# Local attention's later units computed in pairs that share PSUM banks

## The chip, the cores and the metric

The kernel runs on one NeuronCore of a Trainium2 chip, as one program. TensorE (PE) multiplies matrices into PSUM, VectorE (DVE) and ScalarE (ACT) work on PSUM and SBUF, and SyncE (SP) issues nearly all DMA transfers from one queue. The metric is the device time of one execution in microseconds (us); lower is better.

## The reference

Three parts follow each other. The first is attention of 4 batches with 8 heads of width 64, over 512 local positions and 32 global ones:

```python
    s_ll = scale * np.matmul(q_l, k_l.transpose(0, 1, 3, 2))
    mask = np.abs(pos[:, None] - pos[None, :]) <= window      # window = 32
    s_ll = np.where(mask, s_ll, -1000000000.0)
    s_lg = scale * np.matmul(q_l, k_g.transpose(0, 1, 3, 2))
    a_l = sm(np.concatenate([s_lg, s_ll], axis=-1))
    out_l = np.matmul(a_l, np.concatenate([v_g, v_l], axis=2))
```

Beside it 32 global queries see all 544 keys. Its output, 2176 rows of 512, goes through two layers of the same form, `g(x @ w_in) @ w_out` with an inner width of 2048: the first with a leaky activation, the second with `h * relu6(h + 3) / 6`. Everything is in float32.

## The kernel before

**Local units.** A unit is a batch, half of the positions and a pair of heads: 32 units, in the order batch, half, pair of heads. `scores(u)` (L192) multiplies 32 queries at a time by a window of 128 keys, for two heads; heads lie on partitions 0 to 63 and 64 to 127, so these matmuls use 64 rows and 32 columns of the array. The scores of one head go to one PSUM bank (`s0_ps`, `s1_ps`), half of whose 512 columns a unit fills. DVE reads them with the mask and the minimum (L200, four reads a unit), ACT takes the exponential (L204, four a unit), DVE makes the reciprocal of the sums (L206, L208). `transposes(u)` (L215) turns the four 128x128 tiles on PE into one bank, and ACT copies it to `pt` (L217). `values(u)` (L227) multiplies by the values with 128 rows and 32 columns of the array into half of a bank `o_ps`, and DVE scales the result into `xo` (L231). A program's matmul in float32 shows in the trace as two: 16 in the order are 32 in the profile.

**The loop.** `local_units` is a generator. Up to unit 3, and from unit 4 to the last, step k does the transposes of unit k-1 and gives control back; then the scores of unit k, the values of unit k-2, the loads of q and k (L172, L174) for unit k+2 and of v (L179) for unit k+1, and gives control back again. `v_t` has 3 buffers, `q_t` and `k_t` have 4, `p` 2, `xo` 8.

**What runs beside it.** The main program goes through five blocks of rows of the first layer (512, 512, 512, 256 and 384 rows). A block's step s multiplies for `h` (L373), then takes one or two steps of the generator, then multiplies for `y` (L404) with the `g` of two steps earlier; `act` makes `t` and `g` on ACT and DVE (L383, L385, L391, L392). At the end of a block the outputs `xo` of the next block's units are transposed into `xt` (L358, L344, L345), and `y` goes to DRAM (L946, L947, L949). In the first block, which runs in two lanes of 256 columns, the first layer's weights are converted from raw 64-bit words as they come in (L97, L112, L116, L120, L122, L128, L129, mostly DVE); in the blocks after it those of the second layer (`second_weights`, L469 to L501, loads at L97, stores at L478). After the local units the global ones (`global_units`) use the same memory: their loads (`gq`, `gk`, `gv`, L274 to L282) wait until the local units have let go of it.

**Order.** The code is written in that order, and a scheduler with a timeline model places the instructions on each engine; every engine then takes its instructions in that fixed order. PSUM has two pools of four banks; from the first block on, `y_ps` has one pool, and `h_ps`, `s_ps`, `pt_ps`, `o_ps` and `xt_ps` take turns in the other.

## Time and profile before

| | us |
|---|---|
| median of 3 runs (861.42 to 865.12) | 864.32 |
| the profiled execution | 862.99 |
| its span, from the first instruction to the last | 861.2 |
| PE busy in the span | 836.2 |
| DVE busy | 592.5 |
| ACT busy | 418.6 |
| granted TensorE clock, mean share of full speed | 0.986 |

The span lies 1.8 us under the time of the same execution. Busy time of PE counts a matmul from its start to its modelled end, and matmuls overlap; the distance between the starts of two groups tells what a group costs. In the chain of work that ended last each piece is the time that it adds.

### The profile page before, as it was taken

The numbers are of one execution on the slowest core, as the hardware profiler recorded it, in microseconds if no ns is written. First come the engines' busy times: TensorE is split into PE (matmuls) and PEld (weight loads), VectorE is DVE, ScalarE is ACT, GpSimd is POOL, SyncE is SP. The second block draws the span as 40 slices with busy tenths as digits, with TensorE's granted clock in tenths as the row PEclk, the third lists the DMA queues.
The fourth block names the chain that finished last, engine by engine and source line by source line (L and its number), as shares of the span: only waits on it lengthen the run. The fifth ranks groups of instructions, "written<-read, shape, count | busy, mean of one in ns | idle before, by whom it ended". The sixth has DMA issues, their size and how long they took to land.

```text
span 861.2 us, 18367 instructions
## 1 busy us (share of the span) xinstructions
PE 836.2 (97%) x7232; PEld 746.6 (87%) x7232; DVE 592.5 (69%) x1321; ACT 418.6 (49%) x905; POOL 0.2 (0%) x4
## 2 busy tenths in 40 slices
PE   8899999999999999989999999999999999999997
PEld 5678989878778788878999998879999998999996
DVE  4889987566767776677779837779854786854221
ACT  5777665555555555455546523335532343442222
POOL 0000000000000000000000000000000000000000
PEclk7899999999999999999999999999999999999999
DMA  8885664357667656599678626768666887888872
GB/s 309 305 283 181 232 206 139 114 171 249 215 231 246 253 191 210 204 339 327 221 275 286 232 93 220 227 206 275 186 207 217 288 298 222 283 258 262 296 250 77
DMA packets 75204, 199.90 MB, mean 232 GB/s; under 512 B 7792, under 2 KB 23920, under 8 KB 74096
## 3 DMA queue, kind: packets, MB, share of 16 engines
q1 hardware_dynamic: 75024, 198.61, 69.5%
q8 instruction: 57, 0.93, 0.5%
q14 instruction: 27, 0.22, 0.1%
q10 hardware_dynamic: 96, 0.13, 0.1%
HBM read 156.25 MB, written 42.47 MB: 231 GB/s over the span
## 4 chain that ended last, share of the span: by engine, by line
PE 82%; DVE 7%; DMA 6%; ACT 3%; issue 1%; SPq 1%; ACTq 0%
PE h_ps L373 18%; PE y_ps L404 17%; PE o_ps L802 16%; PE k_ps L722 15%; DMA raw<-in_w 4%; PE h_ps L869 4%; PE o_ps L660 4%; PE s_ps L192 2%; PE pt_ps L215 2%; DVE z L120 1%; PE o_ps L227 1%; DMA ws<-wo 1%; DVE z L122 1%; DVE t L385 1%; ACT raw L112 1%
## 5 line engine op out<-in xcount | busy, mean ns | idle before, releaser
L404 PE MATMUL y_ps<-g,wt 128*128 128x256 f32 (+2 forms) x1152 | 212.3, 334 | 5.7 <-ACT g L391 4.0
L373 PE MATMUL h_ps<-xt,wt 128*128 128x256 f32 (+2 forms) x1152 | 209.9, 332 | 3.3 <-ACT wt L128 1.9
L404 PEld LDWEIGHTS y_ps<-g,wt 128*128 128x128 f32 x1152 | 175.3, 189 | 26.5 <-ACT g L391 4.6
L373 PEld LDWEIGHTS h_ps<-xt,wt 128*128 128x128 f32 x1152 | 179.3, 192 | 21.3 <-ACT wt L128 2.1
L802 PE MATMUL o_ps<-ws,gh 128*128 128x256 f32 x784 | 141.5, 284 | 3.3 <-DMA ws<-wo 3.0
L722 PE MATMUL k_ps<-bt,ws 128*128 128x512 f32 (+1 forms) x672 | 137.8, 364 | 0.0
L722 PEld LDWEIGHTS k_ps<-bt,ws 128*128 128x128 f32 x672 | 121.9, 190 | 12.7
L802 PEld LDWEIGHTS o_ps<-ws,gh 128*128 128x128 f32 x784 | 121.9, 192 | 4.8 <-DMA ws<-wo 3.7
L802 PE MATMUL o_ps<-ws,gl 128*128 128x256 f32 x392 | 108.6, 284 | 0.0
L772 DVE TENSOR_TENSOR gl<-far,gh 128x1024 fp32r<-128x1024 f32 (+1 forms) x56 | 60.7, 1088 | 38.5 <-ACT gh L771 38.1
L771 ACT CAST gh<-far 128x1024 fp32r<-128x1024 f32 (+1 forms) x56 | 52.4, 941 | 63.7 <-PE o_ps L802 53.3
L385 DVE SCALAR_TENSOR_TENSOR t<-t,c_sb,h_ps 128x256 f32<-128x256 f32 (+2 forms) x96 | 55.2, 587 | 40.8 <-ACT t L383 40.7
L802 PEld LDWEIGHTS o_ps<-ws,gl 128*128 128x128 f32 x392 | 74.3, 192 | 0.2
L383 ACT ACTIVATE t<-h_ps 128x512 f32<-128x512 f32 (+2 forms) x84 | 42.9, 512 | 56.9 <-PE h_ps L373 55.3
L112 ACT ACTIVATE raw<-raw,quarter_sb 128x512 uint32<-128x512 uint32 x64 | 49.7, 778 | 25.9 <-DMA raw<-in_w 25.8
L391 ACT CAST g<-t 128x512 fp32r<-128x512 f32 (+2 forms) x84 | 44.9, 536 | 34.1 <-DVE t L385 32.1
L392 DVE TENSOR_TENSOR g<-t,g 128x512 fp32r<-128x512 f32 (+2 forms) x84 | 48.9, 584 | 18.2 <-ACT g L391 17.8
L707 ACT ACTIVATE t<-far,half_sb 128x512 f32<-128x512 f32 (+1 forms) x48 | 32.2, 670 | 49.2 <-DVE far L703 49.0
L204 ACT ACTIVATE p<-p,st 128x128 f32<-128x128 f32 x128 | 49.9, 391 | 11.3 <-DVE st L200 10.9
L120 DVE SCALAR_TENSOR_TENSOR z<-z,raw 128x512 uint32<-128x512 uint32 x64 | 43.8, 689 | 3.8 <-ACT raw L112 2.4
L122 DVE SCALAR_TENSOR_TENSOR z<-raw,z 128x512 uint32<-128x512 uint32 x64 | 43.5, 687 | 0.7
L869 PE MATMUL h_ps<-xt,ws 128*128 128x384 f32 x192 | 36.0, 336 | 0.0
(104 smaller groups left out, 880.9 us busy)
## 6 DMA issues: line engine op xcount, KB each, us to landing
ws<-wi SPq DMA_DIRECT2D x80, 512.0 KB, 4.7
ws<-wo SPq DMA_DIRECT2D x72, 512.0 KB, 4.3
raw<-in_w SPq DMA_DIRECT2D x64, 512.0 KB, 5.5
v_t<-in_vE SPq DMA_DIRECT2D x32, 512.0 KB, 5.5
wi<-raw SPq DMA_DIRECT2D x16, 512.0 KB, 3.2
wi<-parts SPq DMA_DIRECT2D x16, 512.0 KB, 5.2
wo<-raw SPq DMA_DIRECT2D x16, 512.0 KB, 3.9
wo<-parts SPq DMA_DIRECT2D x16, 512.0 KB, 4.8
```

The costliest lines, as they stand in the source:

```text
L112: here(nc.scalar.activation(low, low, AF.Relu, bias=quarter_sb, scale=0.9 * 2.0 ** -29))
L120: nc.vector.scalar_tensor_tensor(out=bits, in0=bits, scalar=3, in1=low, op0=ALU.logical_shift_left, op1=ALU.bitwise_or)
L122: nc.vector.scalar_tensor_tensor(out=bits, in0=high, scalar=0x80000000, in1=bits, op0=ALU.bitwise_and, op1=ALU.bitwise_or)
L204: nc.scalar.activation(p[:, n, :], p[:, n, :], AF.Exp, bias=st[:, 1, n:n + 1], scale=-1.0, accum_out=st[:, 2, n:n + 1])
L373: nc.tensor.matmul(ps[:, a:b], lhsT=wts[j][:, 0, wl, 128 * c:128 * c + 128], rhs=xt[c][:, xl, a:b], start=k == 0, stop=k == 3 * NC - 1)
L385: nc.vector.scalar_tensor_tensor(out=t[:, c:d], in0=t[:, c:d], scalar=c1_sb[:, j:j + 1], in1=ps[:, c:d], op0=ALU.mult, op1=ALU.add)
L404: nc.tensor.matmul(y[c][:, a:b], lhsT=wts[j][:, 1, wl, 128 * c:128 * c + 128], rhs=g[:, gl, a:b], start=first, stop=last)
L722: nc.tensor.matmul(bank, lhsT=wt[:, wl, at:at + 128], rhs=bt[x][:, c, xl, 0:w], start=first and k == 0, stop=k == 5, skip_group_check=True)
L771: nc.scalar.copy(hi, src)
L772: nc.vector.tensor_tensor(out=lo, in0=src, in1=hi.bitcast(F32), op=ALU.subtract)
L802: nc.tensor.matmul(bank, lhsT=part[:, jp, 128 * c:128 * c + 128], rhs=wo[:, jp, 256 * wl:256 * wl + 256], start=opens, stop=k == NP // 2 - ...
L869: nc.tensor.matmul(h, lhsT=wt[:, wl, 128 * c:128 * c + 128], rhs=xt[c][:, xl, 0:w], start=k == 0, stop=k == 3 * NC - 1)
```

## The change

The first eight units stay single: the second loop now ends at unit 8 (`SINGLE`), with its last units finished before the next begin. From unit 8 on the units go in twelve pairs. `scores` takes two units: the first unit's scores go to columns 0 to 255 of the two banks, the second's to columns 256 to 511, and all 32 matmuls of the program stand together; the two softmaxes follow. `values` takes two units in the same way, with both results in one bank. A pair takes four steps of the generator: the transposes of the pair before in the first, nothing in the second, the scores of this pair and the values of the one before in the third, the loads in the fourth (v of this pair, q and k of the next). Per engine the number of instructions stays the same, but for q and k of units 10 and 11, which the second loop loads and the first pair loads again. Two units use five banks where they used eight.

```diff
--- before.py
+++ after.py
@@ -33,6 +33,7 @@
 AHEAD = 2
 PRE = 3
 FIRST_UNITS = HP
+SINGLE = 2 * HP
 SKEW = 1
 ZB = 2
 WARM = 8
@@ -178,19 +179,25 @@
             v_t[u] = att.tile([128, 8, 2, D], F32, tag="vE", name="v_t", bufs=3)
             nc.sync.dma_start(out=v_t[u], in_=vE[b, hp, :, 8 * hf:8 * hf + 8])
 
-        def scores(u):
+        def scores(*us):
+            s = [bank("s0_ps"), bank("s1_ps")]
+            for e, u in enumerate(us):
+                b, hf, hp = units[u]
+                q, k = q_t.pop(u), k_t.pop(u)
+                for i in range(2):
+                    for g in range(4):
+                        at = 128 * i + W * g
+                        o = W * (start_of(8 * hf + 4 * i + g) - 12 * hf)
+                        to = 256 * e + 128 * i
+                        for h in range(2):
+                            rows = slice(64 * h, 64 * h + 64)
+                            nc.tensor.matmul(s[h][W * g:W * g + W, to:to + 128], lhsT=q[rows, at:at + W],
+                                             rhs=k[rows, o:o + 128], start=True, stop=True)
+            for e, u in enumerate(us):
+                softmax(u, [x[:, 256 * e:256 * e + 256] for x in s])
+
+        def softmax(u, s):
             b, hf, hp = units[u]
-            q, k = q_t.pop(u), k_t.pop(u)
-
-            s = [bank("s0_ps"), bank("s1_ps")]
-            for i in range(2):
-                for g in range(4):
-                    at = 128 * i + W * g
-                    o = W * (start_of(8 * hf + 4 * i + g) - 12 * hf)
-                    for h in range(2):
-                        rows = slice(64 * h, 64 * h + 64)
-                        nc.tensor.matmul(s[h][W * g:W * g + W, 128 * i:128 * i + 128], lhsT=q[rows, at:at + W],
-                                         rhs=k[rows, o:o + 128], start=True, stop=True)
             p = att.tile([128, 4, 128], F32, tag="p", name="p", bufs=SKEW + 1)
             st = att.tile([128, 4, 4], F32, tag="st", name="st", bufs=4)
             for i in range(2):
@@ -216,22 +223,25 @@
             pt_t[u] = att.tile([128, 4, 128], F32, tag="pt", name="pt", bufs=2)
             nc.scalar.copy(pt_t[u], t.rearrange("p (n q) -> p n q", n=4))
 
-        def values(u):
-            b, hf, hp = units[u]
-            pt, v, rs = pt_t.pop(u), v_t.pop(u), rs_t.pop(u)
+        def values(*us):
             o = bank("o_ps")
-            for i in range(2):
-                for h in range(2):
-                    n = 2 * i + h
-                    for g in range(4):
-                        nc.tensor.matmul(o[W * g:W * g + W, D * n:D * n + D],
-                                         lhsT=pt[:, n, W * g:W * g + W], rhs=v[:, 4 * i + g, h, :],
-                                         start=True, stop=True)
-            x = outs.tile([128, 2, 128], F32, tag="xo", name="xo", bufs=8)
-            nc.vector.tensor_tensor(out=x.rearrange("p i (h d) -> p (i h) d", h=2),
-                                    in0=o[:, 0:256].rearrange("p (n d) -> p n d", n=4),
-                                    in1=rs[:, :, None].to_broadcast([128, 4, D]), op=ALU.mult)
-            xo[b, hf, hp] = x
+            for e, u in enumerate(us):
+                pt, v = pt_t.pop(u), v_t.pop(u)
+                for i in range(2):
+                    for h in range(2):
+                        n = 2 * i + h
+                        to = 256 * e + D * n
+                        for g in range(4):
+                            nc.tensor.matmul(o[W * g:W * g + W, to:to + D],
+                                             lhsT=pt[:, n, W * g:W * g + W], rhs=v[:, 4 * i + g, h, :],
+                                             start=True, stop=True)
+            for e, u in enumerate(us):
+                b, hf, hp = units[u]
+                x = outs.tile([128, 2, 128], F32, tag="xo", name="xo", bufs=8)
+                nc.vector.tensor_tensor(out=x.rearrange("p i (h d) -> p (i h) d", h=2),
+                                        in0=o[:, 256 * e:256 * e + 256].rearrange("p (n d) -> p n d", n=4),
+                                        in1=rs_t.pop(u)[:, :, None].to_broadcast([128, 4, D]), op=ALU.mult)
+                xo[b, hf, hp] = x
 
 
 
@@ -246,7 +256,7 @@
         load_v(1)
         load_v(2)
         yield
-        for lo, hi in ((0, FIRST_UNITS), (FIRST_UNITS, n)):
+        for lo, hi in ((0, FIRST_UNITS), (FIRST_UNITS, SINGLE)):
             if lo:
                 load(lo)
                 load_v(lo)
@@ -264,6 +274,24 @@
                 if 3 <= k + 1 < hi:
                     load_v(k + 1)
                 yield
+        pairs = [(u, u + 1) for u in range(SINGLE, n, 2)]
+        for j in range(len(pairs) + 1):
+            if j:
+                for u in pairs[j - 1]:
+                    transposes(u)
+                yield
+                yield
+            if j < len(pairs):
+                scores(*pairs[j])
+            if j:
+                values(*pairs[j - 1])
+            yield
+            if j < len(pairs):
+                for u in pairs[j]:
+                    load_v(u)
+                    if j + 1 < len(pairs):
+                        load(u + 2)
+            yield
 
     def global_units(att):
         qz = att.tile([128, 2, 128], F32, tag="gqz", name="gqz")
```

On PE in the second block, before (`h_ps` and `y_ps` are the first layer's matmuls, `s_ps` the scores, `o_ps` the values, `pt_ps` the transposes):

```order
L373 MATMUL h_ps<-xt,wt 128x512 x12
L192 MATMUL s_ps<-k_t,q_t 32x128 x16
L227 MATMUL o_ps<-v_t,pt 32x64 x16
L404 MATMUL y_ps<-g,wt 128x512 x12
L373 MATMUL h_ps<-xt,wt 128x512 x12
L215 MATMUL pt_ps<-ident_sb,p 128x128 x4
L404 MATMUL y_ps<-g,wt 128x512 x12
```

and now:

```order
L401 MATMUL h_ps<-xt,wt 128x512 x12
L194 MATMUL s_ps<-k_t,q_t 32x128 x32
L235 MATMUL o_ps<-v_t,pt 32x64 x32
L432 MATMUL y_ps<-g,wt 128x512 x12
L401 MATMUL h_ps<-xt,wt 128x512 x12
L432 MATMUL y_ps<-g,wt 128x512 x12
L401 MATMUL h_ps<-xt,wt 128x512 x12
L222 MATMUL pt_ps<-ident_sb,p 128x128 x8
L432 MATMUL y_ps<-g,wt 128x512 x12
```

Scores and values of a pair stand where those of one unit stood, and every second h group has no attention behind it.

On PE in the first block, from the y group that needs the last converted weights (the first row), before:

```order
L404 MATMUL y_ps<-g,wt 128x256 x4
L373 MATMUL h_ps<-xt,wt 128x256
L192 MATMUL s_ps<-k_t,q_t 32x128 x16
L404 MATMUL y_ps<-g,wt 128x256 x6
L373 MATMUL h_ps<-xt,wt 128x256 x23
L227 MATMUL o_ps<-v_t,pt 32x64 x16
L404 MATMUL y_ps<-g,wt 128x256 x14
L373 MATMUL h_ps<-xt,wt 128x256 x12
```

and now:

```order
L432 MATMUL y_ps<-g,wt 128x256 x4
L401 MATMUL h_ps<-xt,wt 128x256 x13
L194 MATMUL s_ps<-k_t,q_t 32x128 x3
L432 MATMUL y_ps<-g,wt 128x256 x6
L401 MATMUL h_ps<-xt,wt 128x256 x23
L432 MATMUL y_ps<-g,wt 128x256 x14
L194 MATMUL s_ps<-k_t,q_t 32x128 x29
L235 MATMUL o_ps<-v_t,pt 32x64 x32
```

Twelve more h matmuls stand behind that point, and the scores of a pair are split three to 29.

On ACT at the start of the fourth block (`parts` and `raw` belong to the second layer's weights, `ev` is the third block's output, `gp` the global units' exponential), before:

```order
L498 CAST parts<-z 128x2x256
L112 ACTIVATE raw<-raw,quarter_sb 128x512
L383 ACTIVATE t<-h_ps 128x256
L391 CAST g<-t 128x256
L498 CAST raw<-z 128x2x256
L112 ACTIVATE raw<-raw,quarter_sb 128x512
L383 ACTIVATE t<-h_ps 128x256
L391 CAST g<-t 128x256
```

and now:

```order
L526 CAST parts<-z 128x2x256
L411 ACTIVATE t<-h_ps 128x256
L419 CAST g<-t 128x256
L411 ACTIVATE t<-h_ps 128x256
L113 ACTIVATE raw<-raw,quarter_sb 128x512
L411 ACTIVATE t<-h_ps 128x256
L419 CAST g<-t 128x256
```

The steps on raw words moved behind those of the block's first h groups.

## Rows read from the trace of the kernel before

**Rows 1.** The page: busy us, share of the span, instructions.

```profile
PE 836.2 (97%) x7232; PEld 746.6 (87%) x7232; DVE 592.5 (69%) x1321; ACT 418.6 (49%) x905; POOL 0.2 (0%) x4
```

**Rows 2.** Stretches: length; busy PE, PEld, DVE, ACT, POOL (instructions); clock, DMA, GB/s.

```profile
57.60:132.30 74.70, 71.37 (x828) 66.09 (x826) 65.78 (x168) 49.49 (x111) 0.00 (x0) 1.00 0.64 210
...
162.40:266.40 104.00, 104.00 (x947) 83.46 (x946) 70.43 (x189) 55.90 (x138) 0.00 (x0) 1.00 0.61 204
266.40:369.60 103.20, 102.34 (x870) 81.49 (x868) 74.27 (x186) 53.41 (x126) 0.00 (x0) 1.00 0.68 233
369.60:384.60 15.00, 11.75 (x107) 10.05 (x107) 11.25 (x32) 8.67 (x21) 0.00 (x0) 0.89 1.01 323
```

**Rows 3.** The chain that ended last, second block: start, us added, what.

```profile
191.38 0.60 PE s_ps L192 x32
191.98 0.58 PE o_ps L227 x32
192.57 2.95 PE y_ps L404 x12
195.51 2.73 PE h_ps L373 x12
...
211.01 0.44 PE pt_ps L215 x4
```

**Rows 4.** Timeline of PE there: start, first start to last end, what.

```profile
191.31 0.67 PE L192 MATMUL s_ps<-k_t,q_t 64*32 64x128 f32 x32
191.91 0.65 PE L227 MATMUL o_ps<-v_t,pt 128*32 128x64 f32 x32
```

**Rows 5.** Lines of scores and values: ns of one matmul, least/median/most.

```profile
L192 PE MATMUL s_ps<-k_t,q_t x1024: 266/269/420, 4.6 to 335.7; 64*32 64x128 f32 x171
...
L227 PE MATMUL o_ps<-v_t,pt x1024: 217/219/316, 14.2 to 354.8; 128*32 128x64 f32 x171
```

**Rows 6.** Timeline of PE, third block; in brackets idle before, and its end.

```profile
282.44 0.64 PE L192 MATMUL s_ps<-k_t,q_t 64*32 64x128 f32 x16
...
284.48 0.65 PE L227 MATMUL o_ps<-v_t,pt 128*32 128x64 f32 x32
...
300.99 1.19 PE L373 MATMUL h_ps<-xt,wt 128*128 128x512 f32 x4 [0.86 <-DVE t L385]
```

**Rows 7.** The chain, first block, steps on DVE.

```profile
110.44 0.09 DVE rs L208
...
111.72 0.33 DVE xo L231
...
120.26 0.20 DVE p L200
```

**Rows 8.** Groups of DVE, 57.6 to 132.3: count | busy us, mean ns | idle before.

```profile
L129 DVE TENSOR_TENSOR wt<-z,wt 128x512 fp32r<-128x512 f32 x19 | 12.9, 687 | 3.0 <-ACT wt L128 2.6
```

**Rows 9.** Timeline of ACT in the second block: one exponential.

```profile
206.14 0.40 ACT L204 ACTIVATE p<-p,st 128x128 f32<-128x128 f32 x1
```

**Rows 10.** Timeline of DVE there: two sums for the second layer's weights.

```profile
208.94 0.88 DVE L481 TENSOR_TENSOR z<-z 128x256 f32<-128x256 f32 x2
```

**Rows 11.** What ACT waited for, 162.4 to 362: us, times, longest.

```profile
ACT raw L112 <- DMA raw<-in_w: 8.7, 6, 2.7
```

**Rows 12.** Timeline of SP's issues, block three to four.

```profile
356.19 0.33 SPq L274 DMA_DIRECT2D gq<-in_qgT  x1
...
361.04 0.45 SPq L97 DMA_DIRECT2D raw<-in_w  x1
...
370.20 0.57 SPq L97 DMA_DIRECT2D raw<-in_w  x1
```

**Rows 13.** Timeline of PE, block three to four.

```profile
354.34 0.65 PE L227 MATMUL o_ps<-v_t,pt 128*32 128x64 f32 x32
...
378.78 1.93 PE L404 MATMUL y_ps<-g,wt 128*128 128x256 f32 x12 [3.25 <-ACT g L391]
```

**Rows 14.** Timeline of ACT, block three to four.

```profile
376.75 0.75 ACT L112 ACTIVATE raw<-raw,quarter_sb 128x512 uint32<-128x512 uint32 x1 [2.38 <-DMA raw<-in_w]
```

## The prediction

> **What bounds the kernel now.** First the busy times of the page [rows 1]: TensorE (PE) is busy 836.2 us, 97 % of the span. That says which engine to suspect, not where. So second the busy times by stretch [rows 2]; the local units run in the first three. From 57.6 to 132.3 both PE (71.4 of 74.7) and VectorE (DVE, 65.8) are nearly full: the first weights are converted on DVE there. And DVE's records are incomplete: it has 19 low-part subtractions in that stretch [rows 8] where the program's order holds 22 between the same two points, so DVE is fuller than it looks. From 162.4 to 369.6, the second and third block, PE is busy for all but 0.9 us and DVE for about 70 %. From 369.6 to 384.6 PE is busy for only 11.75 of 15 us. Third the chain that ended last, through one step of the second block [rows 3]: it runs on PE alone, so a microsecond taken from PE there is a microsecond of the whole, as long as nothing else becomes late. Twelve wide matmuls take 2.73 us, 0.227 each. The scores of a unit take 0.60, its values 0.58, and the y group behind them 2.95 instead of 2.73: 0.22 is lost in going back to wide matmuls. A unit's excursion costs 0.60 + 0.58 + 0.22 = 1.40 us.
>
> **What a second unit in the same excursion costs.** The 32 score matmuls last 0.67 us from the first start to the last end [rows 4], one of them 0.27 [rows 5]: the starts spread over 0.40, and the rest of the 0.60 is the engine emptying before another shape. For values it is 0.65 less 0.22, 0.43. A second set of 32 behind the first should then add 0.44 each, the spread and the step to the next start. A pair costs 1.40 + 0.88 = 2.28 against 2.80, a saving of 0.52. The ends: 0.22, if the second unit pays its whole 0.60 and 0.58 and only one way back is saved; 0.57, if it pays 0.40 and 0.43 alone. No row shows 64 of one shape at full clock, so I take the value from the spread, to which the rows of the 32 are nearest. Eight transposes in place of four and four: 0.44 for four [rows 3] and nothing lost behind them, no change.
>
> **The change part by part, against the profiled execution** (863.0 us with 861.2 of span, 1.3 under the median of the three runs, 864.3).
>
> Second and third block. By the order there are seven excursions with scores and values of two units and one with values alone, where fourteen and two of one unit stood: 7 x 0.52 = 3.6. The values alone: 2 x (0.58 + 0.22) = 1.60 becomes 0.58 + 0.44 + 0.22 = 1.24, 0.4 saved. One unit's scores were split by three y matmuls: 2.04 us from 282.44 to 284.48 [rows 6] where 0.60 + 3 x 0.227 = 1.28 would do, 0.75 more; the order has no such split there now. Together **4.7 us**, ends 7 x 0.22 = 1.5 and 7 x 0.57 + 0.4 + 0.75 = 5.2. What hides the rest: DVE now reads eight score tiles in a row (8 x 0.20), then two outputs (2 x 0.33) [rows 7], 2.3 us in place of twice 1.15, and ScalarE (ACT) does eight exponentials at 0.40 [rows 9]. The h group before the scores has its DVE step ahead of them in the order; the next h ends a values group, a y and an h group later. PSUM: four banks turn round for h, pt, s and o. Four steps asked for twelve, now for nine, so although a score bank is held for two units' reads, its reuse comes later too. If these covers fail, rival 2 has the price.
>
> A rule speaks against sharing a bank. The Trainium skill, PSUM — Partial Sum Buffer, section Summary: rules for kernel authors, has a reader use a bank other than the one that TensorE writes. By it the first unit's reads wait for the second unit's scores, 0.44 us by my estimate from rows 4 and 5; a sum that priced this on DVE for seven pairs would lose 3.1 us. No row of this kernel can show it, since no bank is shared yet.
>
> First block. DVE has the last weights ready at 132.3, after the softmax of 16 units and the products of 14; in the new order 14 and 12 stand ahead of that point. That takes 2 x (4 x 0.20 + 0.33 + 2 x 0.09) = 2.6 us [rows 7] off DVE's way there. Behind it PE has more: twelve half-wide h matmuls that stood ahead of it (12 x 0.114 = 1.4), and two pairs with one split (2 x 2.28 + 0.5 = 5.1) where two combined and two lone excursions stood (2 x 1.40 + 0.82 + 0.80 = 4.4). Net -2.6 + 1.4 + 0.7 = **-0.5 us**. PE's own savings up to 132.3 count for nothing: DVE covers them. On SP's queue both v loads of a pair now stand together and wait for the values of the pair before; eight raw loads stand behind the second such pair of v loads, two of the last weights behind the third. From those values to the y group that needs the last weights lie 48 y and 48 h matmuls, 11 us by half of 0.227 each; a raw load takes 6.5 to land (issued 370.20 [rows 12], used 376.75 [rows 14]) and its conversion on DVE four steps of at most 0.69 [rows 8], 2.8: it fits with 1.7 us to spare. q and k of units 10 and 11 are loaded twice, since the loop before the pairs loads two units on: 0.74 MB, 3.5 us at the 210 GB/s of that stretch, beside a DMA share of 0.64 [rows 2]: nothing, unless a raw load is late by it. Ends -4 (the second lane may also start about 2 us earlier, two units' scores fewer being ahead of it) and +3.5.
>
> Block three to four. PE waits 3.25 us at 378.78 for ACT [rows 13], and ACT for a raw load that SP issued at 370.20, behind the block's stores [rows 12]; ACT starts on it at 376.75 [rows 14], and that step stands in ACT's row ahead of the t and g of the block's second h. In the new order the t and g of the first h and the t of the second are ahead of the raw step. But the raw load in question is now an earlier one, behind gq; gq waits for the last values, and these now end right ahead of the xt transposes, not a y and an h group (5.7 us) earlier. gq was issued 1.9 us after the last values began [rows 12, 13], raw 4.9 after gq. So raw goes out about 6.5 us after the end of the new values and lands about 13, while PE gets to the end of the second h group after 36 y matmuls (8.2), eight transposes (0.9) and 24 half-wide h (2.7): 12. The load and PE meet within a microsecond or two. Half of the wait is my estimate, **-1.7 us**; ends -4 (wait gone, and with it the time at the lower level of TensorE's clock, 1.2 GHz: 0.89 granted over that stretch [rows 2]) and +4 (the 5.7 later, less the 1.7).
>
> After 384.6 the order changes little, and PE is the chain: the gain is kept. Sum: -4.7 - 0.5 - 1.7 = -6.9, so 856.1 against the profiled 863.0, and **857.4** against the median.
>
> **Rivals.** (1) *Evacuation sets the pace.* The second and third block also carry the conversion of the second layer's weights on DVE and ACT. If these and their raw loads, not PE, set the pace, PE's gain there turns into waiting: ACT waited 8.7 us for raw loads, six times [rows 11], and PE's wait of 0.86 at 300.99 was for DVE's t [rows 6]. Against it: all PE waits of that stretch come to 0.9. With 1.5 of the 4.7 left and no gain at the end: -1.5 - 0.5 = -2, 862.3. The Trainium skill, TensorEngine Tiling (Array Packing), section Performance Considerations, says that tiling speeds up TensorE but not PSUM evacuation. By that rule the first block's rows agree (DVE nearly full), those of the next two do not (DVE at 70 %).
>
> (2) *Slower: the burst delays the next h.* From the end of a pair's scores a read (0.20), eight exponentials (3.2), small steps (0.2), a low part (0.69) and two sums (0.88) [rows 7 to 10] come to 5.2 us until DVE gets to the next t. PE has that h done after 0.58 + 0.44 + 2.95 + 2.73 = 6.7. The margin is 1.5. If a wait for a raw load, up to 2.7 on ACT [rows 11], falls into each of the twelve pairs, each costs 1.2, +14 in all: 864.3 - 6.9 + 14 = 871. It decides, to slower by over 0.5 %, from 0.95 us a pair on. Against it: six such waits in 32 steps.
>
> (3) *More than forecast.* The wait at 378.78 goes whole and the first block gains its 4: -4.7 - 4 - 4 = -12.7, 851.6.
>
> (4) *The scheduler splits the pairs again.* The order shows seven whole pairs in the second and third block, splits in the first alone: no chance of its own.
>
> **How the numbers follow.** Forecast 0.55 (its own range 853.5 to 860.5), rival 1 0.25, rival 2 0.09, rival 3 0.11. A measurement of this kernel tells about 0.5 % from no change: faster means under 860.0. That holds for nine tenths of the forecast (0.50), all of rival 3 and 0.02 of rival 1: 0.63; within: 0.28; slower: 0.09. The range that leaves out 0.2: 852 to 864.
>
> **What would show it.** Right: a pair's excursion in the chain of waits at about 2.3 us (0.60 + 0.44 = 1.04 for scores, 1.02 for values, the y behind them 2.95), the second and third block together 202.5 us instead of 207.2 [rows 2], the first block ending within 1.5 us of 162, PE's wait near 375 under 2. Wrong: scores of a pair near 1.2 (then 1.5 is the gain), PE idle in blocks two and three above 2 us with DVE's t or ACT's g as what ended it (rivals 1 and 2), the raw load behind gq landing 3 us or more after PE's second h group.

## The result, and the profile after

The changed kernel takes 852.30 us (median of 4 runs, 850.47 to 853.92) where the kernel before takes 863.02 (4 runs, 861.42 to 865.12): a ratio of 0.9875, 95 % interval 0.985 to 0.990. Measured again beside the last experiments it took 853.65 against 862.41, 0.9895 (0.9864 to 0.9925). The forecast was 857.4 with a range of 852 to 864. The sign was right and the size short: as a difference -6.9 was forecast, -10.7 and -8.8 were measured. The first median lies only 0.3 inside the range's lower end, and outside the 853.5 to 860.5 that the prediction gave its own forecast.

The profiled execution after has a span of 852.0 us, 9.2 under that of before. The page of the profile after, answering to [rows 1] (busy us, share, instructions), and its summary of the chain that ended last (shares of the span by engine):

```profile
PE 827.0 (97%) x7232; PEld 745.6 (88%) x7232; DVE 592.8 (70%) x1321; ACT 415.2 (49%) x905; POOL 0.2 (0%) x4
...
PE 68%; DVE 12%; DMA 10%; ACT 7%; issue 2%; SPq 1%; ACTq 0%; DVEq 0%
```

The same line of the page of before:

```profile
PE 82%; DVE 7%; DMA 6%; ACT 3%; issue 1%; SPq 1%; ACTq 0%
```

The instructions are the same in number. PE's busy time fell by 9.2, as much as the span; DVE's did not fall, ACT's by 3.4. PE's share of the chain fell too, from 82 to 68 %, but that is one trace: in the changed kernel's other trace (after_again) it is 80 %.

By stretch, from the starts of groups on PE in both traces:

| stretch | before | after | difference | forecast |
|---|---|---|---|---|
| start to the second lane's first h group | 58.1 | 54.4 | -3.7 | |
| from there to the second block | 104.3 | 105.2 | +0.9 | |
| first block together | 162.4 | 159.6 | -2.8 | -0.5 |
| second and third block | 207.2 | 202.7 | -4.5 | -4.7 |
| fourth block to the second layer's first k group | 135.8 | 135.2 | -0.6 | -1.7 |
| the rest | 355.8 | 354.5 | -1.3 | 0 |
| span | 861.2 | 852.0 | -9.2 | -6.9 |

The busy times by stretch after (length; busy PE, PEld, DVE, ACT, POOL with instructions; clock, DMA share, GB/s), answering to [rows 2]:

```profile
54.40:128.90 74.50, 70.36 (x827) 66.08 (x826) 66.77 (x177) 49.71 (x117) 0.00 (x0) 1.00 0.65 224
...
159.60:362.30 202.70, 201.73 (x1818) 166.32 (x1817) 146.50 (x375) 108.95 (x264) 0.00 (x0) 1.00 0.63 216
362.30:379.30 17.00, 14.66 (x127) 13.10 (x126) 12.27 (x33) 8.88 (x23) 0.00 (x0) 0.90 1.02 343
```

In the second and third block PE is still busy for all but 1.0 us. The step into the fourth block still has a hole, of 2.3 us, and the granted clock falls there as before (0.90).

One pair in the second block, on the timeline of PE after (start, first start to last end, what); [rows 4] are the same lines of before:

```profile
199.27 1.16 PE L194 MATMUL s_ps<-k_t,q_t 64*32 64x128 f32 x64
200.36 1.10 PE L235 MATMUL o_ps<-v_t,pt 128*32 128x64 f32 x64
201.39 3.01 PE L432 MATMUL y_ps<-g,wt 128*128 128x512 f32 x12
...
224.27 1.16 PE L194 MATMUL s_ps<-k_t,q_t 64*32 64x128 f32 x64
```

The scores take 1.09 from start to start and the values 1.03; 1.04 and 1.02 were forecast. The next pair's scores start 25.00 us later. Before, two units took 25.49 with the same 48 h and 48 y matmuls between them:

```profile
204.09 0.67 PE L192 MATMUL s_ps<-k_t,q_t 64*32 64x128 f32 x32
...
229.58 0.67 PE L192 MATMUL s_ps<-k_t,q_t 64*32 64x128 f32 x32
```

So a pair saves 0.49 us; 0.52 was forecast.

### The profile page after: what moved, and what is told of

Read it like the earlier page. It is cut to its first block, busy times and chain, and to the rows that moved or that the text cites. A ratio compares the mean times of both kernels' runs of the same rounds, so it can differ in the third digit from the quotient of the medians.

```text
span 852.0 us, 18369 instructions
## 1 busy us (share of the span) xinstructions
PE 827.0 (97%) x7232; PEld 745.6 (88%) x7232; DVE 592.8 (70%) x1321; ACT 415.2 (49%) x905; POOL 0.2 (0%) x4
## 4 chain that ended last, share of the span: by engine, by line
PE 68%; DVE 12%; DMA 10%; ACT 7%; issue 2%; SPq 1%; ACTq 0%; DVEq 0%
PE o_ps L830 17%; PE k_ps L750 15%; PE y_ps L432 12%; PE h_ps L401 11%; DMA raw<-in_w 6%; PE h_ps L897 4%; PE o_ps L688 4%; DVE z L121 2%; DVE t L413 2%; ACT p L211 2%; PE s_ps L194 2%; DVE z L123 1%; ACT raw L113 1%; DMA ws<-wo 1%; DVE g L420 1%
## 5 line engine op out<-in xcount | busy, mean ns | idle before, releaser
L432 PE MATMUL y_ps<-g,wt 128*128 128x256 f32 (+2 forms) x1152 | 208.8, 332 | 5.8 <-ACT g L419 3.1
L432 PEld LDWEIGHTS y_ps<-g,wt 128*128 128x128 f32 x1152 | 177.2, 191 | 23.1 <-ACT g L419 3.5
L799 ACT CAST gh<-far 128x1024 fp32r<-128x1024 f32 (+1 forms) x56 | 52.4, 942 | 63.3 <-PE o_ps L830 53.2
```

The costliest lines, as they stand in the source:

```text
L432: nc.tensor.matmul(y[c][:, a:b], lhsT=wts[j][:, 1, wl, 128 * c:128 * c + 128], rhs=g[:, gl, a:b], start=first, stop=last)
L799: nc.scalar.copy(hi, src)
```

## The experiments

Two questions were open. Theory A of the first block: it got faster because units 8 and 9 start only after units 4 to 7 are done (the drain), so that less stands ahead of the second lane; theory B: because units go in pairs. And for the later blocks: does PE save changes of shape, or does sharing banks free something? All runs in one table; lane and block are start times in the profiled execution, and the kernel before was timed on the same chip beside each group of four.

| kernel | lane | 2nd block | 2nd + 3rd | median | before beside it | ratio (95 %) |
|---|---|---|---|---|---|---|
| changed kernel | 54.4 | 159.6 | 202.7 | 852.30 | 863.02 | 0.9875 (0.985 to 0.990) |
| after_again | 55.6 | 159.8 | 202.3 | 853.65 | 862.41 | 0.9895 (0.9864 to 0.9925) |
| e_drain | 54.5 | 164.6 | 208.7 | 866.33 | 863.96 | 1.0035 (1.0019 to 1.0051) |
| e_early | 53.9 | 157.5 | 207.7 | 858.62 | 862.41 | 0.9951 (0.9933 to 0.9969) |
| e_late | 59.5 | 166.8 | 204.5 | 862.88 | 863.96 | 0.9991 (0.9967 to 1.0015) |
| e_late_once | 57.6 | 160.6 | 203.6 | 860.56 | 862.47 | 0.9965 (0.9942 to 0.9988) |
| e_turn | 53.8 | 157.2 | 204.5 | 855.46 | 863.96 | 0.9908 (0.9882 to 0.9934) |
| e_own | 56.4 | 162.3 | 208.7 | 862.99 | 863.96 | 0.9992 (0.9972 to 1.0012) |
| e_once | 54.9 | 159.5 | 201.8 | 855.01 | 862.47 | 0.9901 (0.9872 to 0.9930) |
| e_pool_after | 54.9 | 160.1 | 201.6 | 854.46 | 862.47 | 0.9897 (0.9868 to 0.9925) |
| e_hyb | 53.2 | 156.2 | 202.5 | 851.59 | 862.47 | 0.9871 (0.9842 to 0.9900) |
| e_gpool | 53.5 | 158.8 | 202.8 | 858.46 | 862.41 | 0.9943 (0.9920 to 0.9965) |
| e_best | 54.8 | 157.8 | 202.3 | 857.07 | 862.41 | 0.9927 (0.9903 to 0.9952) |

Runs of one kernel differ by several us (the kernel before: 859.2 to 868.8 over 29 runs), so the profiled execution is not always the middle one: that of e_late took the longest of its 12 times, that of e_late_once the shortest. Whole times are compared by medians, stretches by traces.

### The changed kernel again

> The changed kernel unaltered, beside the three below on one chip, as their measure and to see how far its stretches repeat: second block from 159.6 within 1 us, second and third block 202.7 within 1, in all 851 to 854.

It came as expected. The second block starts within 0.2 us of the first trace, the two blocks after it take 202.3 instead of 202.7, and the wait into the fourth block is again 2.3. The start of the second lane moves by 1.2 from run to run: single readings of it carry little. Taken together they do: it lies between 53.2 and 56.4 in the eleven traces of kernels that drain at unit 8, between 57.6 and 59.5 in the three of kernels that do not.

### The drain alone

```diff
-        for lo, hi in ((0, FIRST_UNITS), (FIRST_UNITS, n)):
+        for lo, hi in ((0, FIRST_UNITS), (FIRST_UNITS, 2 * HP), (2 * HP, n)):
```

> The kernel before with one edit: the loop over single units ends its pipeline at unit 8 as it does at unit 4 (units 4 to 7 run out, their last values included, before unit 8 starts). No unit is paired. Theory A (the first block got faster because units 8 and 9 start later, not because they are a pair): the second lane opens at about 54.5 us instead of 58.1, the block ends at about 160 instead of 162.4, the second and third block stay at 207, in all about 2.5 us less than before. Theory B (the pairing itself freed it): the lane opens near 58, the block ends at 162.4 or later, since a fill and a drain are added, and the time is that of before or up to 1.5 us more.

Neither theory held. The lane opens early, as A says. The lane's first h group on the timeline of PE, in the kernel before:

```profile
58.11 2.06 PE L373 MATMUL h_ps<-xt,wt 128*128 128x256 f32 x15 [0.27 <-DVE xt L345]
```

In the changed kernel:

```profile
54.41 1.80 PE L401 MATMUL h_ps<-xt,wt 128*128 128x256 f32 x13
```

With the drain alone:

```profile
54.53 1.68 PE L373 MATMUL h_ps<-xt,wt 128*128 128x256 f32 x12
```

But from there to the second block it takes 110.1 us instead of 104.3, so the block ends 2.2 us later than before, and the whole is slower by 2.4 us. The timeline of PE at the end of its first block shows where some of it went:

```profile
153.05 0.49 PE L215 MATMUL pt_ps<-ident_sb,p 128*128 128x128 f32 x3
...
156.62 0.33 PE L215 MATMUL pt_ps<-ident_sb,p 128*128 128x128 f32 x1
156.88 0.40 PE L192 MATMUL s_ps<-k_t,q_t 64*32 64x128 f32 x2
157.21 0.33 PE L215 MATMUL pt_ps<-ident_sb,p 128*128 128x128 f32 x1
157.47 0.44 PE L192 MATMUL s_ps<-k_t,q_t 64*32 64x128 f32 x14
...
159.07 0.65 PE L227 MATMUL o_ps<-v_t,pt 128*32 128x64 f32 x32
159.65 2.29 PE L404 MATMUL y_ps<-g,wt 128*128 128x256 f32 x17
```

The drain costs the single units a step of the generator, and two units must be made up for ahead of the block's last transposes. Transposes one by one between pieces of scores take 0.26 each from start to start, where four in a row take 0.35: from 153.05 to 159.65 there are two units' transposes, scores and values and ten y matmuls, worth 4.3 us at the rates of single units (2 x 0.35 + 2 x 0.60 + 2 x 0.58 + 10 x 0.12), in 6.6. That is 2.3 of the 5.8 us; 1.2 more are the scores of two units (0.60 each) that the drain moved behind the lane's start, and some 0.4 the transposes of one unit that moved with them; the other 1.9 were not traced.

### Pairs in the first block alone

```diff
+        LAST = 4 * HP
-        pairs = [(u, u + 1) for u in range(SINGLE, n, 2)]
+        pairs = [(u, u + 1) for u in range(SINGLE, LAST, 2)]
```

From unit 16 on single units follow without a drain.

> Pairs in the first block alone (units 8 to 15), single units from 16 on, without a drain at 16. If the first block's gain needs drain and pairs together (the drain alone lost 2.2 us there, the pairs from 16 on cannot bring it): second block from 159.6 within 0.7, as in the changed kernel; second and third block 207 to 210, since PE pays single excursions again, and in all 859 to 862. If the pairs in the first block do nothing without those behind: second block from 162 on, 863 or more.

The first expectation held in the main: 858.62, 3.8 us under the kernel beside it. The second block starts at 157.5, 2.1 us earlier still than in the changed kernel (about 0.5 of it is one unit's scores that come behind that point here, 0.5 more the lane's earlier start), and the next two blocks take 207.7, about the 207.2 of before. With e_drain this says of the first block: the drain opens the second lane early, and with pairs, one excursion for two units, that lead is kept to the end; with single units it is not. Pairs in the first block without the drain were not tried, so how the lead divides between the two is not shown.

### Pairs from unit 16 on

```diff
-SINGLE = 2 * HP
+SINGLE = 4 * HP
```

> The changed kernel with the pairs from unit 16 on instead of unit 8; units 4 to 15 run singly as before. Theory A and theory B both: the first block as before (lane near 58, end at 162.4 within 1). Excursions theory (PE pays for each change of shape): second and third block 202.7 to 203.5 instead of 207.2, the step into the fourth block 1 us less, in all 5 to 6 us less than before and some 2.8 to 4 more than the changed kernel. Were the whole gain one thing that starts with the drain at unit 8, the second and third block would also stand near 207 here.

The two blocks took 204.5, not 207, so PE's saving there is real without the drain at 8 (and 203.6 in the next run). But the whole gained nothing that can be measured: the first block ended 4.4 us late, and ScalarE waited longer for raw loads of weights. On SP's queue the doubled loads of q and k, here of units 18 and 19, stood among the last raw loads. The test took only the doubles away:

```diff
-                if lo and k + 2 < n:
+                if lo and k + 2 < SINGLE + 2:
```

> Pairs from unit 16 on as in e_late, with q and k of units 18 and 19 loaded once: they were loaded twice right ahead of the last raw loads of the first layer's weights. Queue theory (these four loads pushed the last raw loads back; that, not the pairs, took e_late's gain): the y group that needs the last weights comes at 132 to 134 instead of 137.2 us, the second block starts at 162.5 to 164 instead of 166.8, in all 858 to 860. If it starts at 166 again, they did not, and the gain is lost to something in the pairs themselves.

ScalarE's waits for raw loads from 20 to 140 us (us, times, longest), in e_late:

```profile
ACT raw L113 <- DMA raw<-in_w: 14.9, 9, 2.9
```

And in e_late_once:

```profile
ACT raw L113 <- DMA raw<-in_w: 8.8, 8, 2.5
```

SP's issues in e_late (start, us), where the loads of q and k from 125.42 on are the doubled ones and the raw load behind them is the first of the last four:

```profile
125.42 0.33 SPq L173 DMA_DIRECT2D q_t<-in_qT  x1
125.97 0.82 SPq L175 DMA_DIRECT2D k_t<-in_kE  x1
126.88 0.38 SPq L98 DMA_DIRECT2D raw<-in_w  x1
```

The block started at 160.6 instead of 166.8. Not all of the 6.2 is the doubles' doing: 1.9 of it stood already at the second lane, and 1.8 more at the raw loads issued at 104.56 (100.84 without), ahead of any doubled load. In the medians, each against the kernel before beside it, e_late gains 1.1 us and e_late_once 1.9: the difference of 0.8 lies within their intervals, so that a cost of the doubled loads is not shown. Pairs from 16 on bring 1.9 us by the median where 5 to 6 were expected, within a scatter of 7 us in this kernel's runs. With the 3.8 of e_early that makes 5.7 for the two parts of a change that gained 8.8 and 10.7 as a whole: by the medians the parts do not add up to it, and why stays open.

### Scores and values in turn

```diff
+            for e in range(2):
+                scores(banks=s, es=[(e, us[e])])
+                values(o=o, es=[(e, vs[e])])
```

> The changed kernel, with the scores and values of a pair in turn: scores of one, values of one, scores of the other, values of the other, in the same shared banks, and all reads of these banks after them as in the changed kernel. Only back to back is undone. Excursions theory (PE pays for each change of shape, 0.60 and 0.58 for a set with its change against about 0.45 for a second set behind the first): a pair's excursion 2.36 to 2.4 us up to the y group instead of 2.12, second and third block 204.5 to 205 instead of 202.7, in all about 3 us more than the changed kernel. Rival (the gain comes from the one way back to wide matmuls and from fewer banks in use): no more than 0.5 us between the two.

The excursions theory held in the two blocks. Timeline of PE, second block:

```profile
198.08 0.67 PE L194 MATMUL s_ps<-k_t,q_t 64*32 64x128 f32 x32
198.68 0.65 PE L236 MATMUL o_ps<-v_t,pt 128*32 128x64 f32 x32
199.26 0.67 PE L194 MATMUL s_ps<-k_t,q_t 64*32 64x128 f32 x32
199.86 0.65 PE L236 MATMUL o_ps<-v_t,pt 128*32 128x64 f32 x32
200.44 3.01 PE L448 MATMUL y_ps<-g,wt 128*128 128x512 f32 x12
...
223.35 0.67 PE L194 MATMUL s_ps<-k_t,q_t 64*32 64x128 f32 x32
```

The excursion takes 2.36 us instead of 2.12, the period is 25.27 instead of 25.00, and the two blocks take 204.5. So of the 0.49 that a pair saves, 0.27 comes from standing back to back (two changes between the shapes of scores and of values less) and 0.22 from going out once instead of twice. The whole does not show the 3 us that were expected: 855.46 is 8.5 under the kernel before beside it, where the changed kernel gained 10.7 and 8.8, and the intervals overlap. The first block ended 2.4 us earlier here than in the changed kernel; from the fourth block on this trace took 2.5 us longer, with the same order of work there, and what made it so was not traced. The early end of the first block was taken up in e_hyb.

### Banks of their own

```diff
-            s = [bank("s0_ps"), bank("s1_ps")]
             for e, u in enumerate(us):
+                s = [bank("s0_ps"), bank("s1_ps")]
```

> The changed kernel, with scores of each unit in banks of its own (four a pair instead of two); values share their bank. The order then has most pairs' scores in two pieces, 24 and 8 (by its count, with 15 y matmuls between), since four banks go round for everything. Excursions theory: the extra piece costs a change of shape and a way back, 0.4 to 0.6 a pair, second and third block 205.5 to 206.5 instead of 202.7; in all 4 to 6 us more than the changed kernel, thus near 857. Rival (sharing a bank holds reads up, so that own banks would win): second and third block at or under 202.7.

The direction was right, the size larger: 208.7, 6.0 us more than with shared banks, and all of the change's gain is gone (862.99). Timeline of PE:

```profile
203.59 1.10 PE L196 MATMUL s_ps<-k_t,q_t 64*32 64x128 f32 x48
204.62 3.72 PE L434 MATMUL y_ps<-g,wt 128*128 128x512 f32 x15
208.27 0.64 PE L196 MATMUL s_ps<-k_t,q_t 64*32 64x128 f32 x16
208.84 1.10 PE L237 MATMUL o_ps<-v_t,pt 128*32 128x64 f32 x64
...
229.35 1.10 PE L196 MATMUL s_ps<-k_t,q_t 64*32 64x128 f32 x48
```

The four banks that go round don't hold two units' scores beside h, so the order puts the last quarter behind 15 y matmuls. The period is 25.76, 0.76 more than in the changed kernel: one more change to scores (1.03 + 0.57 instead of 1.09) and one more way back. Sharing a bank is thus not the aim but the means: it lets the pair stand together.

The Trainium skill, PSUM — Partial Sum Buffer, section Summary: rules for kernel authors, has a reader take another bank than the one that TensorE writes. By it the shared banks should hold DVE's reads up. The timeline of DVE in the changed kernel beside the pair of 199.27 shows that in DVE's order as it stands they would have come no sooner:

```profile
200.01 0.75 DVE L413 SCALAR_TENSOR_TENSOR t<-t,c_sb,h_ps 128x512 f32<-128x512 f32 x1 [0.94 <-ACT t L411]
201.45 0.69 DVE L420 TENSOR_TENSOR g<-t,g 128x512 fp32r<-128x512 f32 x1 [0.69 <-ACT g L419]
202.06 0.28 DVE L207 CUSTOM_DVE_ANT_0 p<-s_ps,mask_sb 128x128 f32<-128x128 f32 x1
```

The first read starts 1.6 us after the last score (199.27 + 1.16), because t and g of the h group stand ahead of it, and in no pair of the two blocks does it start sooner. The rule's price, estimated at 0.44 us a pair in the prediction, was not paid here.

### Loads once, and on another queue

e_once is the changed kernel with the edit of e_late_once. e_pool_after has only the issuing engine changed (and so for `k_t` and `v_t`):

```diff
-            nc.sync.dma_start(out=q_t[u], in_=qT[b, hp, :, 256 * hf:256 * hf + 256])
+            (nc.gpsimd if u >= 2 * HP else nc.sync).dma_start(out=q_t[u], in_=qT[b, hp, :, 256 * hf:256 * hf + 256])
```

> The changed kernel with q and k of units 10 and 11 loaded once: four transfers (0.74 MB) less on the queue of SP, early in the second half of the first block; the order of TensorE is the same. If doubled loads cost nothing (the prediction's value): within 0.5 us of the changed kernel, the second block starting at 159.6 within 0.5. If they hold up the raw loads of weights behind them: waits of ScalarE for raw loads (5.0 us from 20 to 140) fall, the second block starts 1 us or more earlier.

> The changed kernel with q, k and v of units 8 on issued from the queue of GpSimd, which does nothing else, instead of SP's; the order of TensorE is the same. If raw loads of weights still stand behind v loads that wait for a buffer: with these gone the waits of TensorE for wt between 60 and 140 us (4.2 us in the changed kernel) fall below 2, the second block starts near 157.5, and the wait at the start of the fourth block (2.3 us) falls, in all 848 to 850. If not the queue but DMA bandwidth or VectorE sets the first block: 159.6 and 852 as before.

Neither moved the first block: 159.5 and 160.1, against 159.6 and 159.8 of the changed kernel's two traces. The doubled loads of units 10 and 11 cost nothing where they stand, as the prediction had it, and SP's queue is not what sets the first block.

### The first block in turn, and the global loads elsewhere

e_hyb takes e_turn's order in the first block and the changed kernel's behind it. e_gpool issues the five loads of a global unit from GpSimd, as in:

```diff
-            nc.sync.dma_start(out=q, in_=qgT[hp])
+            nc.gpsimd.dma_start(out=q, in_=qgT[hp])
```

e_best has both and loads q and k once.

> Pairs in turn (scores, values, scores, values) in the first block alone, as in e_turn, and back to back from the second block on, as in the changed kernel. If e_turn's earlier start of the second block (157.2 instead of 159.6) came from its order, it comes again, and with blocks two and three at 202.7 the whole is 2 to 2.5 us under the changed kernel, 850. If it was a matter of when raw loads landed in that run, the second block starts at 159 to 160 and the time is 852.

The early start came again (156.2), with 202.5 behind it. It is more than the lane's start: from there to the second block the three versions with turns in the first block take 102.9 to 103.4 us, the five with the changed kernel's order there 104.1 to 105.3, and PE's waits for weights in that stretch come to 2.6 us in place of 3.3 to 4.2. Why the weights come sooner was not traced. In the median, 851.59, that is within the intervals of the changed kernel's two measurements: no gain is shown.

> The changed kernel with the five loads of each global unit (q, masked q, k, v) issued from GpSimd's queue instead of SP's. Queue theory for the wait at the start of the fourth block (2.34 us for ScalarE's g, behind a raw load issued at 359.25 us, which stood on SP behind gq waiting for the last values): the raw load goes out 2 to 3 us sooner and lands before gk and gv, the wait falls under 0.7, from the fourth block's start to the first k group of the second layer 2 us less (133.2 instead of 135.2), in all 850. Bandwidth theory (the transfers share one set of DMA engines, busy all through that stretch): raw lands as late, or the wait comes back at the first global scores, 852.

Neither theory's number came: 858.46, 4.8 over the changed kernel beside it, for 850 and 852. The raw load went out at 355.00 instead of 359.25 and the first wait shrank to 0.86, but ScalarE waited 4.85 us for a later raw load, and PE stood for 5.8. Busy times of the step into the fourth block (columns as above):

```profile
361.60:376.40 14.80, 13.17 (x127) 11.52 (x125) 11.27 (x32) 8.76 (x23) 2.19 (x4) 1.00 1.01 358
```

The two waits on the timeline of PE (in brackets idle before, and its end):

```profile
371.86 1.69 PE L432 MATMUL y_ps<-g,wt 128*128 128x256 f32 x12 [0.86 <-ACT g L419]
...
391.36 2.08 PE L432 MATMUL y_ps<-g,wt 128*128 128x256 f32 x8 [5.81 <-ACT g L419]
```

What ScalarE waited for ahead of each, on its timeline:

```profile
371.40 0.41 ACT L419 CAST g<-t 128x256 fp32r<-128x256 f32 x1 [0.99 <-DMA x<-ev]
...
387.41 0.76 ACT L113 ACTIVATE raw<-raw,quarter_sb 128x512 uint32<-128x512 uint32 x1 [4.85 <-DMA raw<-in_w]
```

The first is no longer for a raw load at all, but for a store of `ev`, the third block's output; the account of the prediction below comes back to it. Ahead of the second, the steps that the raw word lets loose stand in DVE's row in front of the next t, which starts 2.9 us after ScalarE has the load:

```profile
390.29 0.47 DVE L413 SCALAR_TENSOR_TENSOR t<-t,c_sb,h_ps 128x256 f32<-128x256 f32 x1
```

14.8 us instead of 17.0 for the step, then 125.6 instead of 118.2 up to the second layer. In the step the DMA engines are busy all through (share 1.01). The Trainium skill, DMA: Bandwidth & Descriptors, section Rules for kernel authors, says that transfers issued from two engines still share the same DMA engines; the row agrees, with 358 GB/s where the changed kernel's step moves 343 from one queue. The late raw load went out on SP at 379.07, where that of the changed kernel went out at 376.86: SP had waited 9.6 us for a store of `parts` to land, 15.6 us after the store's issue (10.4 in the changed kernel). The load was then used 8.3 us after its own issue instead of 6.6. Both were slower, then; which transfers slowed them was not settled.

> All three that could help at once: pairs in turn in the first block (e_hyb), single loading of units 10 and 11, and the global loads on GpSimd's queue. If the two effects add (first block 156.5, wait at the fourth block gone): 847.5 to 849.5. If the first block's start of e_hyb was within the spread of the changed kernel and the queue gives nothing: 851 to 853.

857.07, with the wait of e_gpool in it (5.1 us here): the effects don't add. No version tried is shown to beat the changed kernel.

## Why the prediction was right, and where it was off

**What bounds it: right.** PE's chain of the second and third block was the place, and a microsecond taken from PE there was one of the whole: all waits of PE in those 202.7 us come to 1.0. Of the total, the sum is 2.3 us short: 2.3 in the first block and 1.3 of scatter in the rest, less 1.1 at the fourth block and 0.2 in the second and third. That the time still fell into the range is in part luck, since these errors cancel in part.

**Second and third block: right, -4.5 for -4.7.** The pair's saving was 0.49 for 0.52, and e_turn shows its two halves. Seven pairs make 3.4 of it. The rest, some 1.1, is the values alone and the one unit that had been split [rows 6]; these two were not measured apart. One unit's transposes (0.4) besides fall behind the start of the second block where they stood ahead of it before (60 of the trace's before, 64 after, between these two points), so that without this shift the first block would have gained 0.4 less and these two 0.4 more. One cover failed: the four banks. At the end of the second block the transposes' bank waited for DVE's t, 0.97 us, about as long as the wait at 300.99 that went [rows 6]. Timeline of PE:

```profile
250.35 1.10 PE L235 MATMUL o_ps<-v_t,pt 128*32 128x64 f32 x64
252.41 0.66 PE L386 MATMUL xt_ps<-ident_sb,xo 128*128 128x128 f32 x4 [0.97 <-DVE t L413]
```

**First block: the step that failed, -2.8 for -0.5.** Its sum was -2.6 on DVE up to the last weights, +1.4 for twelve h matmuls behind them and +0.7 for excursions. The group that needed the last weights, at 132.29 before, stands at 128.93 after, 3.4 us earlier instead of 2.6; behind it 30.7 us follow where 30.1 did, +0.6. So the +0.7 was right and the +1.4 does not exist: the traces have the same number of h matmuls behind that group, 72 of the trace's in both. The lists of the order show it too, with 1 + 23 + 12 before and 13 + 23 now; that twelve more stand there is a misreading. And DVE, which the sum took as the limit up to 132, is none at that point any more. The last wait for weights after is this, on PE's timeline:

```profile
121.97 3.38 PE L432 MATMUL y_ps<-g,wt 128*128 128x256 f32 x24 [0.20 <-ACT wt L129]
```

From 122 us on PE alone sets the end of the block. The prediction had the cause in its lower end ("the second lane may also start about 2 us earlier") and left it out of the sum; it was 3.7 in the one trace and 2.5 in the other. What it did not see is that the drain alone would have lost this again.

**Step into the fourth block: the second step that failed, -0.6 for -1.7.** The sum had the raw load land 13 us after the last values and PE end its second h group 12 after them. PE did (12.2, from 353.1 to 365.3), but the load was used on ScalarE 15 us after them, at 368.15: it had gone out when forecast (6.1 us after them for 6.5) and took 8.9 us instead of 6.5. It came 2.8 us behind PE's second h group, just short of the 3 that the prediction names as a sign of being wrong, and PE's wait is over the 2 that it names as a sign of being right. Even so the load is not what ended PE's wait of 2.34 for g. The trace of the changed kernel puts ScalarE's own wait ahead of that g down to a step of the raw word on DVE. PE, then ACT:

```profile
372.06 2.21 PE L432 MATMUL y_ps<-g,wt 128*128 128x256 f32 x12 [2.34 <-ACT g L419]
...
368.15 0.77 ACT L113 ACTIVATE raw<-raw,quarter_sb 128x512 uint32<-128x512 uint32 x1 [2.36 <-DMA raw<-in_w]
...
371.60 0.41 ACT L419 CAST g<-t 128x256 fp32r<-128x256 f32 x1 [2.40 <-DVE z L123]
```

In the second trace, where PE waits 2.29 us at the same place, the same g starts before that step has ended and before DVE's next t begins. What ended ScalarE's wait there is a store. ACT, then DVE:

```profile
371.29 0.40 ACT L419 CAST g<-t 128x256 fp32r<-128x256 f32 x1 [2.31 <-DMA x<-ev]
...
370.65 0.68 DVE L123 SCALAR_TENSOR_TENSOR z<-raw,z 128x512 uint32<-128x512 uint32 x1
371.32 0.47 DVE L413 SCALAR_TENSOR_TENSOR t<-t,c_sb,h_ps 128x256 f32<-128x256 f32 x1
```

The code says why: `ev`, the third block's output, has the tag of `g` and so takes one of its three buffers, and a later g can't be written there until the stores have landed:

```python
            r = work.tile([128, 2, 512], F32, tag="g", name="ev", bufs=LAG + 1)[:, :, :n]
```

The store in the chain of the second trace, from its issue to its landing, with what hung on it (start, us added, what):

```profile
361.63 9.55 DMA x<-ev
...
371.29 0.41 ACT g L419
...
371.74 1.85 PE y_ps L432 x12
```

In the first trace ScalarE's sequencer waits for the same stores until 371.5, and DVE's step ends within 0.05 us of that. e_once, e_pool_after and e_hyb show the store as the cause too. With the raw load alone ScalarE would have had g at about 369.6 by my estimate (the t behind the raw step starts at 368.82 and takes 0.37, g 0.41), when PE came to it, at 369.7: the sum put the right load beside PE and left out the stores. No run moved these stores or gave `ev` a buffer of its own, so that what the step would gain by it is not shown.

**The rest, -1.3:** the change has nothing there. The same stretch took 354.0 us in the changed kernel's other trace and 356.2 in e_once, so this is scatter.

**Rivals.** Rival 1 (evacuation sets the pace, no gain at the end) was wrong in size but may have a grain: the chain that ended last goes through raw loads and conversion in the third block after, up to the wait of 2.34; in the second trace it is on PE there. Rival 2 did not show: no h of the second or third block waited for its t behind a pair. Rival 3's number, 851.6, lies nearest to the result, but by half of its mechanism: the wait did not go, and the first block gave 2.8 instead of 4.

## What to carry to other kernels

Where PE is the chain, count its changes of shape: work of one narrow shape put back to back saves a part of each change, and sharing a bank is worth it when there are too few banks to keep the pieces together. A drain of a software pipeline is paid for with a step; it is worth it only if the steps behind it have room, so read the last stretch before the next deadline, not only the one that the drain frees. When a wait is to go, list all that it hangs on, the buffer too: here a store from a buffer shared by tag held the wait when the load in question had come. Of a late load, price the row of instructions behind it on the engine that uses it (2.9 us on DVE in e_gpool). And a transfer that is moved forward on busy DMA engines can be followed by others that land later, so measure the stretch behind it as well.

## What the runs showed of the hardware

- A change between the shapes of scores (64 rows, 32 columns) and values (128 rows, 32 columns) costs about 0.14 us each way: 0.27 a pair for two more of them (e_turn). 64 matmuls of one shape take 1.09 and 1.03 us where 32 take 0.60 and 0.58.
- A single transpose between pieces of another shape takes 0.26 us from start to start, one of four in a row 0.09 (e_drain).
- After the wait of 2.34 us the next twelve y matmuls of the trace took 2.21 us from first start to last end (1.85 in the second trace, after 2.29), after a wait of 0.86 the same twelve took 1.69 (e_gpool). The granted clock of the two stretches was 0.90 and 1.00 of full speed, the first thus a mixture of the levels of 1.2 and 2.4 GHz.
